# Attention and expert-mixture kernel on one core: every step issued in a newly listed order

## The chip, the cores and the metric

The kernel runs on one core of a Trainium2 chip. A core has five engines, each with a queue of its own that is worked off strictly in order: TensorE (PE in the profile, with its weight loads as PEld), VectorE (DVE), ScalarE (ACT), GpSimd (POOL) and SyncE (SP), which here only issues transfers. The metric is the device time of one execution in microseconds, as a median of several runs.

## The reference, cut to what matters

Two layers follow each other. The first is linear attention over 8 batches of 8 heads with 576 positions; the second takes its output as `x` and mixes four causal attention experts, of which each position uses two.

```python
def phi(x):
    proj = np.einsum('bhsd,df->bhsf', x, w_phi)
    proj = proj - np.max(np.abs(proj), axis=-1, keepdims=True)
    return np.concatenate([np.exp(proj), np.exp(-proj)], axis=-1)
q_p, k_p = phi(q), phi(k)
kv, z = np.einsum('bhsf,bhsd->bhfd', k_p, v), np.sum(k_p, axis=2)
x = np.einsum('bhsf,bhfd->bhsd', q_p, kv) / (q_p @ z + 1e-6)      # heads side by side: 512 features
...
for e in range(4):                                               # second layer
    q, k, v = x @ wq[e], x @ wk[e], x @ wv[e]
    a = causal_softmax(q @ k.T / sqrt(64))
    out += gate[e] * (a @ v @ wo[e])                             # gate: softmax over the two best of x @ w_gate
```

## The kernel before, in words

The work of the first layer is cut into 32 pairs of heads (`p`), that of the second into 8 batches with two groups of two experts each (16 units `n`). Each part is a Python generator, called a stream here, that emits the instructions of one step and then yields the engine of its next step:

- `stream_k`, `stream_tails`: projections of the keys (L501), maximum and subtraction on VectorE (L566, L569), exponentials on ScalarE (L305).
- `stream_q`: projections of the queries (L501), copies out of PSUM, a maximum over partitions on GpSimd (L713), subtraction on VectorE (L715), exponentials on ScalarE.
- `stream_kv`: the products of keys and values (L642 with `v_in`) and the sums of the keys (L654). From pair 4 on the key sums are first added up by accumulating transfers that GpSimd issues into `zs` (L331, L582).
- `stream_n`: denominators (L740) and numerators (L751), then a division on VectorE.
- `stream_s`: projections of the second layer (L294), scores (L871), masks on GpSimd (L979), maxima (L992, L996), subtraction (L1000), exponentials, sums (L1012, L1038).
- `stream_t`: scores times values (L1067) and the output projection (L294), stored by SP.
- loads: `load_v` has one buffer, `v_in`: the load of pair `p` may begin only after the products of pair `p-1`. `q_in` and `k_in` have two buffers.

TensorE works with four tilings of its array, which the profile prints after the names: 128*128 (second-layer projections, transposes), 64*128 (first-layer projections and scores), 128*32 (all products that give 32 columns) and 64*32 (the tails, L607). A run of neighbouring groups of one tiling is followed by a change to another.

Nothing in the kernel orders the work but two literal strings. `ORDER` has one character for each of 3,118 steps; the character's code minus 48 is the place, in the list of streams still open, of the stream that steps next. A stream that ends leaves the list, and a new one (a copy out of PSUM, say) is appended. `SIDES` has one digit for each of 520 copies that either ScalarE (0) or VectorE (1) can make.

```python
for c in ORDER:
    s = self.streams[ord(c) - 48]
    if isinstance(st.eng, tuple):
        st.eng = st.eng[int(next(sides))]
    slot = sorted(self.psum[st.tag], key=lambda kt: self.last.get(kt[0], (0.0, ''))[0])[:st.n]
```

The costs in `class Plan` (`run`, `transfer`, `blocked`, `change_cost`) decide nothing here but which of the eight free PSUM banks a step takes: the one whose last use the costs put earliest. `in_order` makes each engine keep the listed order. `keep_warm` issues 21 small matmuls in seven steps, on data that no result uses.

Of the kernel before, what the change touches and what calls it, by code (L numbers as in the profile page):

```python
# [45 lines left out]
WARM = 0   # L46
# [22 lines left out]


ORDER = (
    r'1110049B32894DDBBDCB726C8D99E1B8DF7GD4FEHDH000C=EDBF5CBBB9DC1934DEFE==E98H2=HIHHCED168E<=A541F<77DBIFJCEAE6AHH'
    r'HIC93941HB<D<E<AGBC<===G<E9GGDAGGDCF9529<GD6GH9B48KEI13F<0;7EA6CKCECG@<<BIH<B;B8IGJE8?A@EF:AE57C7@A2J:?JHHF:18'
    r'6830ADEBDB;;;BFC6CC277GGE?LF?K@FBF2G@8::3BIHEF;;:DIH@?:5ADHIGBF7:HGH::EB;?FAEEE76C8C@CJI>IC?B0;<<<<95IE884B8FB'
    r'F9F<GHH02IEGHAB3?966B>81;A>8=8CB6EB9E99BD>A=>DABAAAB;88C8A?8841>;7CC;@G5?7EEJC>D;3;88KIJODEDDJICHBB;;;;;AF80:E'
    r'FFBCE>?EHEH;AAG:6FF?DC8DD8D;2;5C@@ACBBB8:MIJBI::<IAGIC@FBH99F869FHDB8DCECB83CFBFBC088=DFEECBC8:68I8BFF70HG7IID'
    r'CG8D?5=B<GH6C4:99B2ECMEBEJA8J9886=GJD?>778CMI<HJKI>I<I@<BG39E9C18IHE<A@=8=?E?9G8857?7?EHAJJF083882HGF8ICDHC8DD'
    r'998:C6:GJHI>?I<:JG<1J:7IGH7J:KJGD:?<<BB:BE>@C>;GIIF>L;8>GJGIIJ;8<:=8:HJGHGGJ:IF::LGGK?I=N8=5:=>@K802GQJMM>F:I<'
    r':<0CEEBK=CFE::CFDCDDCJBICDCJCE=D9;;IJHJ<ICIKFHDF4883DD<8<G<<=BBBEI=CCDCDGEFEHGE8BB8D6A8>:I<C5:@@JJ@JEECIAD6BFI'
    r':JK:9FLH9MCLCIJGDHAF9BFAHD8IHBCIE880DH=28BHCB9;ADA@@CA@C@AEL@HB=ECD9;JJBBJD<BGFC;38772J7GF88GG?K=FD<CF895?==A3'  # L80
    r'=8EB888E67FE18D@KHJ@<0E@BCB28=E9988BBDIJID8DGB8848AF<B6<6EE57:7::G=HICLHE3DJDI:::;<BJGC>HD9GHG>B>GADEAF>EEE=8D'
    r'880@C?=B:98:DAF6DIEH8G8GBD9<:::GHHG7BB?NICL5H7B6N=EE;BGC@FI;G=E9?BDJEEBA:<::MGKKDBCG:GC=CD@BIGLMGKFBJH<G:=1348'
    r'8>?EI8IHCA=B;C<<<B>B28>:8:>>>JD>DL8DCBFKJE8::C=<FKEA5G8@:<=HFJHH9<>99AM=6HD?EK==K3@88028K7CJCLFNMKD>?<F?8G887?'
    r'26I88I<AGCC?KJBG<?G=99?8F>H?>F88883AH?E9=I5=F170GIJ@EIKG<=A<DE=HE<7LDB9=<M808<;;C<C6FDCDA99<GGDJ8G@KK7DL85N2GB'
    r'38JGNMGNMHFE?GAG6F><<7:::48E:FF8F8CDFB=E:E:FIJKJ>8FCCCI89B9JIBHI>8:FDDC@D88A::EA3D7F:LFHK8:<II7PHFG?A?@KL@H=5B'
    r'KNN8:6::MPOAMAOGE;E:80:F28E241AKLIJIIFAEEB08=B>ECE8EF:;;89GHH8@@>?5HE6?HI?IHCFBE?B<<<<<GE6BDB>AC?E=CBCB?>:9;@9'
    r'JJ>>A89E=:GJGLKGJ@38087J<887F=88G8LKC:?8G?:KHL<FJH@69@9P95SADQNOQ3A8788O8OMQQPR<@NQN<MEB889ADF>HCIAJB>=99II>GD'
    r'E8<H2=CD8<FFCD7AA7888?D7FCJEA?0?812:503D4=>GA?EBI::H:<BLNELK6:ACBH6K9GAJG9A?I7I7<JH<HF??IAG?NJHIL<GM::<<E@>J28'
    r'88>FE8?A6KKGCFIJFG5MIK8;@EL;N3KPK8L:<NQNL>;:8L:84F0RP=L@:>>OPK:K:FO@KAF:::8LPMKHDFNFG:HFGLKJMK<IGGEEGE=E82CEDC'
    r'FDCC;E;D8F89::I;FL8LF=GGEC5:HN:<<=L=PDOSJBBJDE@<IBJ<DA<BEIMI?F=D9KE99AB01886OCEJGCE6IKACJAM>FDEBGLJGBHMFA@>883'  # L90
    r'@<I?FCB<DH<A888IG8875AGI7IDCMDE>IEK>C>BFCJ=<B??A?D999FFGE8GFEE3088882A8FFC<677F8GF8FA999AG6E<818248>I?EHJK7H<H'
    r'7ED5A>MFIENN>NEDFHE6HK388A<FFFC>DGG:;:99GDG;::::IHK<CJ<GFJKL??FFIKJEH8CB6I;DFKKDFJJ8:8<:::JJNMM8>57:GKBGQ6FP::'
    r'::HQRBD@3880808>E@R>K@C8HIKC=ID:HDEBFDBDBBDCADBBBHHG1<C@7875::9BCBA9C@@7AB<A64?@I;L?KA?HC?L?@IJ<G>;>F;;;==ACAB'
    r'F>DIE9KH9G9?FBBH<IFC;82=8FC73=M@D117B?B778M0;;;MJ@>JMLN>6IJBG9;=6@A>J?HCEG>6@6@@<46DEE53>G;;?>DAG;5II@:E?B=A:;'
    r'A;;797B>66660056CDF>D:B9C9DB<B9B668BA<3CB583B?A4;B@@?8;533BCB:@4A?<8=2224;B?@C;@6=2024C?64111336331D;F>DF?C5C1'
    r';CCC>?:133A?C93B5@3AD3AB39FB@C<78AA3>C?:9?3?B;=8<29@;?><?<A>><211877A;:A>=;>4;42;A3C<1=C?C>@000:8;?::>:7@75008'
    r'8;<4444=475EB<0C:007222?5>=822CF41;@18@;7?777D:9:;;;:01>679==6636800;<=B?95?04<7;761=000>6=6>><=89=54002<;<9;3'
    r'9:77674734607420224700<;02232=5722901>::509;7761008866838<8:50:97086880500100:8865857757957:996657161660005?=='
    r'90064444=A=7<71=1??119;588::276679;697672141125541121171101141311114144;;322=2:1591427717235100230553431131212'
    r'100=>45210<<0;;01168224224344034023200'  # L100
# [17 lines left out]
class Plan:  # L118
# [4 lines left out]
    def __init__(self):  # L123
        self.warm, self.busy = False, []
        self.tiling = None
        self.rings = [0.0, 0.0]
# [30 lines left out]
    def run(self, eng, cost, w=(), r=(), rows=128, tiling=(128, 128), port=False):
# [15 lines left out]
        if eng == 'POOL' and port:
            t = max(t, self.pairs + 215.0)
        if eng == 'POOL' and self.shared[0] < t < self.shared[1]:
            t = self.shared[1]
# [1015 lines left out]
```

## Time and profile before

| | us |
|---|---|
| median of three runs | 584.94 |
| range of the runs | 583.61 to 585.01 |
| span of the profiled execution, first to last instruction | 582.0 |
| TensorE busy in it | 568.9 |
| VectorE busy in it | 533.0 |
| ScalarE busy in it | 454.3 |
| GpSimd busy in it | 290.3 |

The profiled execution has a span of 582.0 us; what lies outside the span brings it to the run's time, 2.9 us by the median. An engine's busy time counts its instructions, not the issuing of transfers. A matmul's end is modelled, so that small gaps between pipelined matmuls don't show as idle: the distance between the starts of neighbouring groups is the better measure of what a group takes.

### The profile page before, as it was taken

The page shows a single profiled execution, that of the slowest core. Times are in us where ns is not written, and L with a number is a line of the kernel's source. Part 1 is how long each engine was busy: PE and PEld are TensorE (multiplying, and loading weights), DVE is VectorE, ACT ScalarE, POOL GpSimd, SP SyncE. Part 2 cuts the span into 40 slices and gives each one's busy share as a digit, 9 for nine tenths or more (in the row PEclk, how much of TensorE's full clock was granted, in tenths as well). Part 3 has the DMA queues.
Part 4 walks back from the last instruction along what each step waited for, and adds up shares of the span by engine and source line. Part 5 has one row for each costly group of instructions (what it writes and reads, how often), then busy time and mean ns, then how long its engine had stood idle before and what let it go on. Part 6 is the DMA issues. An engine that isn't in the chain of part 4 may idle for free.

```text
span 582.0 us, 19187 instructions
## 1 busy us (share of the span) xinstructions
PE 568.9 (98%) x7655; PEld 439.9 (76%) x7655; DVE 533.0 (92%) x1150; ACT 454.3 (78%) x1109; POOL 290.3 (50%) x223
## 2 busy tenths in 40 slices
PE   7998999999999999999999999999999999999997
PEld 5664797678785779667876878867888677878886
DVE  7999899999999998999898989989999998898894
ACT  4999888878897969868878877979778678677562
POOL 3737472666336474465554466446635367331430
PEclk9999999999999999999999999999999999999999
DMA  6579656653445753593664663565646432311012
GB/s 164 151 180 212 119 119 141 148 116 95 95 122 136 180 121 55 139 229 76 153 139 102 156 133 107 100 156 134 131 125 148 116 87 46 89 57 43 1 56 110
DMA packets 55049, 69.74 MB, mean 120 GB/s; under 512 B 29232, under 2 KB 32688, under 8 KB 54960
## 3 DMA queue, kind: packets, MB, share of 16 engines
q1 hardware_dynamic: 48368, 49.58, 29.3%
q0 software_dynamic: 6272, 18.35, 19.9%
q8 instruction: 60, 0.98, 0.7%
q10 hardware_dynamic: 320, 0.59, 0.4%
q14 instruction: 29, 0.24, 0.1%
HBM read 35.59 MB, written 14.55 MB: 86 GB/s over the span
## 4 chain that ended last, share of the span: by engine, by line
PE 86%; DVE 6%; DMA 4%; ACT 2%; issue 1%; SPq 0%; ACTq 0%; DVEq 0%
PE ps_c L294 31%; PE ps_c L501 10%; PE ps_c L751 10%; PE ps_c L642 10%; PE ps_c L1067 7%; PE ps_c L871 7%; PE ps_c L740 5%; DMA v_in<-in_v_dram 2%; PE ps_c L654 2%; PE ps_c L607 2%; DVE s L1000 1%; DMA q_in<-in_qt_dram 1%; PE ps_c L1038 1%; DVE u L715 1%; DVE max L1012 1%
## 5 line engine op out<-in xcount | busy, mean ns | idle before, releaser
L713 POOL PARTITION_ALL_REDUCE mx<-u x64 | 145.1, 2289 | 68.2 <-DVE s L1000 17.5
L294 PE MATMUL ps_c<-x,qk 128*128 128x256 f32 (+1 forms) x768 | 108.0, 298 | 0.6 <-DVE yl L298 0.6
L294 PEld LDWEIGHTS ps_c<-x,qk 128*128 128x128 f32 x768 | 102.7, 189 | 4.4 <-issue 0.9
L996 POOL PARTITION_ALL_REDUCE max<-top x16 | 57.7, 3605 | 39.3 <-DVE top L992 18.1
L979 POOL TENSOR_SCALAR_AFFINE_SELECT s<-s 128x256 f32<-128x256 f32 (+1 forms) x80 | 46.4, 626 | 57.3 <-ACT s L303 45.3
L305 ACT ACTIVATE ek<-ek 128x1024 f32<-128x1024 f32 x64 | 67.9, 1061 | 8.0 <-DVE ek L569 7.3
L303 ACT COPY s<-ps_c 64x64 f32<-64x64 f32 (+4 forms) x141 | 52.9, 434 | 17.7 <-PE ps_c L871 17.4
L1000 DVE TENSOR_TENSOR s<-s,max 128x1152 f32<-128x1152 f32 (+4 forms) x80 | 65.5, 853 | 0.6 <-POOL max L996 0.6
L642 PE MATMUL ps_c<-ek,v_in 128*32 128x256 f32 x1024 | 61.7, 381 | 2.2 <-DMA v_in<-in_v_dram 2.2
L305 ACT ACTIVATE s<-s 128x384 f32<-128x384 f32 (+4 forms) x80 | 57.7, 742 | 7.4 <-DVE s L1000 7.1
L294 PE MATMUL ps_c<-yh,wo 128*128 128x256 f32 (+1 forms) x256 | 52.9, 300 | 0.0
L331 POOL DMA_DIRECT2D zs<-ekt x28 | 23.7, 845 | 58.3 <-DVE zs L582 22.4
L642 PEld LDWEIGHTS ps_c<-ek,v_in 128*32 128x32 f32 x1024 | 31.5, 110 | 25.4 <-DMA v_in<-in_v_dram 2.9
L303 ACT COPY u<-ps_c 128x256 f32<-128x256 f32 (+1 forms) x107 | 40.5, 401 | 11.4 <-PE ps_c L501 10.9
L715 DVE TENSOR_TENSOR u<-u,mx 128x576 f32<-128x576 f32 x64 | 48.9, 779 | 0.4 <-POOL mx L713 0.4
L294 PE MATMUL ps_c<-vg,x 128*128 128x260 f32 x384 | 49.0, 285 | 0.2 <-ACT s L303 0.2
L331 POOL DMA_DIRECT2D zs<-ek x28 | 25.4, 906 | 46.1 <-ACT ek L305 29.6
L294 PEld LDWEIGHTS ps_c<-vg,x 128*128 128x128 f32 x384 | 47.1, 188 | 1.2 <-issue 0.5
L1067 PE MATMUL ps_c<-s,vs 128*32 128x320 f32 (+4 forms) x896 | 46.8, 357 | 0.2 <-DVE ek L569 0.2
L501 PE MATMUL ps_c<-q_in,wf 64*128 64x256 f32 (+1 forms) x256 | 42.8, 430 | 3.6 <-DMA q_in<-in_qt_dram 3.2
L566 DVE TENSOR_REDUCE pmax<-ps_c 128x4 f32<-128x512 f32 x64 | 42.4, 681 | 3.8 <-PE ps_c L501 3.3
L305 ACT ACTIVATE mx<-u 128x576 f32<-128x576 f32 x64 | 43.3, 687 | 2.3 <-DVE u L715 2.0
(132 smaller groups left out, 1350.3 us busy)
## 6 DMA issues: line engine op xcount, KB each, us to landing
zs<-ek POOLq DMA_DIRECT2D x28, 512.0 KB, 5.3
out_dram<-ot SPq DMA_DIRECT2D x32, 288.0 KB, 3.0
q_in<-in_qt_dram SPq DMA_DIRECT2D x60, 144.0 KB, 3.6
k_in<-in_kt_dram SPq DMA_DIRECT2D x64, 128.0 KB, 3.4
v_in<-in_v_dram SPq DMA_DIRECT2D x32, 256.0 KB, 3.3
kvd<-kvt SPq DMA_DIRECT2D x104, 48.0 KB, 2.4
kv<-kvd SPq DMA_DIRECT2D x26, 192.0 KB, 2.5
zs<-ekt POOLq DMA_DIRECT2D x28, 128.0 KB, 3.3
```

The source lines that it names most:

```text
L294: nc.tensor.matmul(o, a, b, start=start, stop=stop, skip_group_check=True)
L303: nc.scalar.copy(o, i)
L305: nc.scalar.activation(o, i, func, **kw)
L331: nc.gpsimd.dma_start(o, i, accum_op=ALU.add)
L501: nc.tensor.matmul(o, a, b, start=True, stop=True, skip_group_check=True)
L642: nc.tensor.matmul(o[g, 0:2], v_in[:, 4 * h + t, k:64:2], ek[:, t, :, h, :].rearrange("p c (w f) -> p c w f", w=4), start=False, stop=t == ...
L713: nc.gpsimd.partition_all_reduce(M, U, 128, bass_isa.ReduceOp.absmax)
L715: dve(S, [uk], [mk], port=True).tensor_tensor(out=U, in0=U, in1=M, op=ALU.subtract)
L751: nc.tensor.matmul(ps[g:g + 32, 0:n], kvi[:, 2 * k + (h ^ p % 2), 32 * c:32 * c + 32], P_[h][c][:, s0:s1], start=c == 0, stop=c == 1, skip ...
L996: nc.gpsimd.partition_all_reduce(big.rearrange("p e s -> p (e s)"), top.rearrange("p e s -> p (e s)"), 128, bass_isa.ReduceOp.max)
L1000: dve(2 * (S - 128 * j), [('d', x, j)], [('max', z)], 1.11, True).tensor_tensor(out=block(s_, j, None, rows(j)), in0=block(s_, j, None, ro ...
L1067: nc.tensor.matmul(ps[r:r + 32, q0 - s0:s1 - s0], vs[:, j, 128 * g + 64 * e + k:128 * g + 64 * e + 64:2], ss[x][:, e, o + q0:o + s1], star ...
```

## The change

Both strings are replaced, with the same lengths of 3,118 and 520. The steps are the same on each stream, in the same order within a stream; what differs is how the streams are interleaved, and on which engine some copies run. The seven steps of `keep_warm` are now counted (`WARMS = 7`), where the loop before ended when the first `x` was there, which was also after seven. The costs of `Plan` are changed as well (a table for changes of tiling, a normal distribution for VectorE's wait behind GpSimd, two rings for transfers), and with them the choice of PSUM banks. A default argument `p=p` is added in `stream_n`, where `p` can't have moved on by then.

```diff
-WARM = 0 
+WARMS = 7
-EXIT = 95.0
-ENTRY = {'F': 102.0, 'R': 99.0, 'S': -31.0, 'C': 23.0, 'Q': 10.0}
+CHANGES = {'CR': 160.0, 'CS': 160.0, 'CF': 190.0, 'CQ': 220.0, 'FC': 100.0, 'FQ': 90.0, 'FR': 95.0, 'FS': 92.0, 'RF': 105.0, 'RC': 100.0, 'RS': -85.0, 'RQ': 105.0,
+           'SR': 50.0, 'SF': 118.0, 'SC': 118.0, 'SQ': 136.0, 'QC': 255.0, 'QR': 245.0, 'QF': 245.0, 'QS': 255.0}
...
 ORDER = (
-    r'1110049B32894DDBBDCB726C8D99E1B8DF7GD4FEHDH000C=EDBF5CBBB9DC1934DEFE==E98H2=HIHHCED168E<=A541F<77DBIFJCEAE6AHH'
...
+    r'11112221111307@16ABAA@7A02@5@BCB776F64;05ABD@DC2B7B7CJ@BI@3;FDCCECC1277@;@EDGB0F6;@I@5;KKB<@EAKGHGJDG@3E;DAF6;'
...
 SIDES = (
-    r'11110000111111000000001000011100000000110101100000001010001000000010010000110000000000000010000000000000000000'
...
+    r'11100000000100100000001000111000000000011000000001101000000000000000000100000000000000000000000000000000000000'
...
-        while ('x', WARM, PARTS[1][0]) not in done:
+        for _ in range(WARMS):
             yield Step('PE')
```

Read character by character against the streams' steps, the two strings give these orders. Each engine but VectorE and ScalarE has as many steps as before: TensorE 658, GpSimd 219, SP 297.

Neighbouring TensorE groups of different tiling (A: 128*128, B: 64*128, C: 128*32, D: 64*32):

| from, to | A B | A C | A D | B A | B C | B D | C A | C B | C D | D B | D C | all |
|---|---|---|---|---|---|---|---|---|---|---|---|---|
| before | 12 | 23 | 9 | 30 | 27 | 4 | 14 | 43 | 3 | 6 | 10 | 181 |
| after | 7 | 21 | 9 | 26 | 19 | 6 | 11 | 40 | 1 | 4 | 12 | 156 |

Within B, a projection of the first layer directly before or after a group of scores: 24 times before, 44 after.

Copies on VectorE: 73 before, 55 after. Those on ScalarE: 447 and 465. The difference of 18 is mostly copies out of PSUM of 256 to 320 columns, `u` (6), `s` (4), `kkh` (4) and `ot` (3).

The `keep_warm` steps: before, three at the head of TensorE's list, three behind the key projections of pair 1 (L501), one behind the transposes of pair 2 (L665); after, all seven at the head.

TensorE work listed between the end of one pair's L642 products and the start of the next pair's, where it is under 5.5 us (each sum made of the start-to-start durations of such groups in the trace of the kernel before, as all sums of listed work here): before, pair 1 4.9, pair 5 4.2 and pair 13 5.1; after, pair 1 4.9, pair 2 5.3, pair 3 4.4, pair 11 4.9 and pair 21 4.6. Pairs 5 and 17 have 4.2 and 9.8 us before, 10.8 and 13.5 after.

TensorE work listed between the last step on another engine and the TensorE step that uses its result, as a median: exponentials of a query pair to its denominators, 3.9 us before and 6.9 after; last add into `zs` to its use, 5.1 and 6.4; `y` to the output projection, 3.2 and 6.8; last sum on VectorE to L1038, 1.8 and 2.8; exponentials of a key pair to L642, 14.4 and 13.3.

## Rows read from the trace of the kernel before

**Rows 1.** The page's first part: busy us, share of the span, instructions.

```profile
PE 568.9 (98%) x7655; PEld 439.9 (76%) x7655; DVE 533.0 (92%) x1150; ACT 454.3 (78%) x1109; POOL 290.3 (50%) x223
```

**Rows 2.** Windows: length, busy us of each engine (instructions), granted clock, DMA share, GB/s.

```profile
9.00:560.00 551.00, 546.78 (x7384) 420.69 (x7381) 513.66 (x1087) 442.75 (x1080) 289.73 (x219) 1.00 0.51 120
...
9.00:40.00 31.00, 30.49 (x531) 20.48 (x531) 30.04 (x60) 29.45 (x56) 19.51 (x12) 1.00 0.61 163
80.00:160.00 80.00, 79.51 (x1038) 62.22 (x1039) 76.28 (x156) 65.80 (x160) 43.20 (x35) 1.00 0.54 121
```

**Rows 3.** Waits of TensorE: who waited for whom, total us, times, longest.

```profile
PE ps_c L501 <- DMA q_in<-in_qt_dram: 3.2, 2, 3.0
PE ps_c L642 <- DMA v_in<-in_v_dram: 2.2, 2, 1.7
```

**Rows 4.** Timeline of TensorE's matmuls, 302 to 324 us: start, length, line, operands, tiling, count.

```profile
302.60 0.67 PE L740 MATMUL ps_c<-mx,kv 128*32 128x288 f32 x8
...
303.68 0.39 PE L871 MATMUL ps_c<-qh,kkh 64*128 64x256 f32 x2
...
307.92 0.42 PE L871 MATMUL ps_c<-qh,kkh 64*128 64x320 f32 x2
...
308.46 0.36 PE L871 MATMUL ps_c<-qh,kkh 64*128 64x448 f32 x2
...
312.65 1.16 PE L501 MATMUL ps_c<-wf,k_in 64*128 64x128 f32 x16
313.65 0.60 PE L501 MATMUL ps_c<-q_in,wf 64*128 64x256 f32 x4
...
318.18 0.70 PE L740 MATMUL ps_c<-mx,kv 128*32 128x288 f32 x8
...
319.15 0.43 PE L654 MATMUL ps_c<-zs,ones 128*32 128x128 f32 x8
...
322.91 1.06 PE L501 MATMUL ps_c<-wf,k_in 64*128 64x128 f32 x16
323.89 1.33 PE L294 MATMUL ps_c<-x,qk 128*128 128x256 f32 x9
```

**Rows 5.** The same timeline, 363 to 385 us.

```profile
363.12 1.05 PE L501 MATMUL ps_c<-wf,k_in 64*128 64x128 f32 x16
363.92 0.39 PE L871 MATMUL ps_c<-qh,kkh 64*128 64x320 f32 x2
...
364.44 0.36 PE L871 MATMUL ps_c<-qh,kkh 64*128 64x448 f32 x2
...
383.73 1.06 PE L501 MATMUL ps_c<-wf,k_in 64*128 64x128 f32 x16
384.62 0.71 PE L501 MATMUL ps_c<-q_in,wf 64*128 64x320 f32 x4
```

**Rows 6.** The chain that ended last, at two places: start, us, what it waited on.

```profile
50.25 5.73 DMA v_in<-in_v_dram
...
247.40 6.25 DMA v_in<-in_v_dram
```

**Rows 7.** Timeline of GpSimd before those two places: issues of accumulating transfers.

```profile
48.92 0.89 POOL L331 DMA_DIRECT2D zs<-ek  x1 [1.19 <-ACT ek L305]
...
245.45 0.89 POOL L331 DMA_DIRECT2D zs<-ek  x1 [3.83 <-ACT x L303]
```

**Rows 8.** The tile v_in, all 32 loads: from issue to landing.

```profile
DMA to landing us min/median/max: 2.5/3.3/6.3
```

**Rows 9.** Groups by line and shape: a VectorE copy; ScalarE's longest exponential, from the page.

```profile
L315 DVE COPY u<-ps_c 128x320 f32<-128x320 f32 x11 | 5.2, 481 | 0.4 <-PE ps_c L501 0.4
...
L305 ACT ACTIVATE ek<-ek 128x1024 f32<-128x1024 f32 x64 | 67.9, 1061 | 8.0 <-DVE ek L569 7.3
```

**Rows 10.** Timeline of TensorE at the start: the small matmuls of keep_warm.

```profile
1.06 1.14 PE L294 MATMUL ps_c<-warm 128*128 128x128 bf16 x9 [1.06 <-DVE col L338]
...
11.51 0.68 PE L294 MATMUL ps_c<-warm 128*128 128x128 bf16 x9
```

More of the change, by code (lines that the diff above doesn't have):

```diff
@@ L1 @@
+import math
 from contextlib import ExitStack
@@ new lines, in expected, with shape_kind @@
+def expected(x, hold):
+    x = 4.0 * math.floor(x / 4.0 + 0.5)
+    if not -2400.0 <= x < 5792.0:
+        return 0.0
+    a, b = (hold - x) / SPREAD, (-LEAD - x) / SPREAD
+    below, at = (lambda z: 0.5 * (1.0 + math.erf(z / 2 ** 0.5))), (lambda z: math.exp(-0.5 * z * z) / (2 * math.pi) ** 0.5)
+    return max(0.0, (hold - x) * (below(a) - below(b)) + SPREAD * (at(a) - at(b)))
+def shape_kind(t):
+    return ('C' if t[0] == 128 else 'Q') if t[1] < 128 else 'F' if t[0] == 128 else 'S' if len(t) > 2 else 'R'
@@ L64, in change_cost @@
 def change_cost(a, b):
-    if a is not None and a[:2] == b[:2]:
+    if a is None or a == b:
         return 0.0
-    kind = ('C' if b[0] == 128 else 'Q') if b[1] < 128 else 'F' if b[0] == 128 else 'S' if len(b) > 2 else 'R'
-    return EXIT + ENTRY[kind]
+    return CHANGES[shape_kind(a) + shape_kind(b)]
 ORDER = (
-    r'1110049B32894DDBBDCB726C8D99E1B8DF7GD4FEHDH000C=EDBF5CBBB9DC1934DEFE==E98H2=HIHHCED168E<=A541F<77DBIFJCEAE6AHH'
-    r'HIC93941HB<D<E<AGBC<===G<E9GGDAGGDCF9529<GD6GH9B48KEI13F<0;7EA6CKCECG@<<BIH<B;B8IGJE8?A@EF:AE57C7@A2J:?JHHF:18'
@@ L74 @@
[L74 to L78, printed above, removed]
@@ L134, in __init__ @@
         self.pairs = 0.0
+        self.issued = False
         self.done = set()
@@ L151, in clocked, with blocked @@
         return 2 * cost if slow else cost
-    def blocked(self, t):
-        return max([b - t for a, b in self.pool if a < t < b], default=0.0)
+    def blocked(self, t, cost):
+        late = 0.0
+        for a, b, lo in self.pool:
+            if b - a > 1000:
+                late = max(late, expected(t - a, b - a))
+            elif lo < t < b:
+                late = max(late, b - t)
+        if self.pool and not self.issued and t < self.pool[-1][0] and late <= 200.0:
+            self.free['POOL'] += max(0.0, t + cost - self.pool[-1][0] - 140.0)
+        return late
     def run(self, eng, cost, w=(), r=(), rows=128, tiling=(128, 128), port=False):
@@ L169, in run @@
         if eng == 'DVE' and port:
-            cost += self.blocked(t)
+            cost += self.blocked(t, cost)
             self.shared = (t, t + cost)
             self.pairs = t + cost
[L173 to L176, printed above, removed]
+        if eng == 'POOL':
+            if port:
+                t = max(t, self.pairs + 215.0)
+            if port > 1000 and self.issued:
+                lo = t - 250.0 if t - self.free[eng] < 60 else t
+            else:
+                if self.shared[0] < t < self.shared[1]:
+                    t = self.shared[1]
+                lo = t
         end = t + cost
@@ L194, in transfer @@
         self.free[eng] = t + issue
+        if eng == 'POOL':
+            self.issued = True
         ring = int(eng == 'POOL')
-        self.rings[ring] = max(self.rings[ring], t + issue + 650.0) + cost
-        end = self.rings[ring] + (1500.0 if ring else 1150.0)
+        lead, rate, tail, share = RINGS[ring]
+        (a, b), (c, d) = self.rings[ring], self.rings[1 - ring]
+        x = max(b, t + issue + lead)
+        if x > b:
+            a = x
+        b = x + cost * rate
+        if c <= x < d:
+            b = min(x + cost * rate / share, d + max(0.0, cost * rate - share * (d - x)))
+        self.rings[ring] = (a, b)
+        end = b + tail
         for k in r:
@@ L741, in stream_n @@
                                          P_[h][c].rearrange("p (a b i) -> p b a i", b=2, i=32)[:, half], start=c == 0, stop=c == 1, skip_group_check=True)
-            plan.spawn(fractions('d', p, ps, pk, 1e-6, xf, ['xf'], (lambda: all(('xd', p - 1, s0) in done for s0, s1 in PARTS)) if p else None, ('rb', p)))
+            plan.spawn(fractions('d', p, ps, pk, 1e-6, xf, ['xf'], (lambda p=p: all(('xd', p - 1, s0) in done for s0, s1 in PARTS)) if p else None, ('rb', p)))
             for s0, s1 in PARTS:
```

67 lines of the change are left out of this document (38 added, 29 removed).

## The prediction

> **What bounds the kernel now.** I read the page's first part, then the windows, then TensorE's waits, then TensorE's timeline. The first part shows TensorE busy for 98% of the span, VectorE for 92%, ScalarE for 78% and GpSimd for 50% [rows 1]. The windows show where TensorE's 13.1 us of idle time are: between 9 and 560 us it is busy for 546.78 of 551.00 us, so only 4.2 us are idle there [rows 2]; the other 8.9 us are the start, where 3.2 us are waits for the first query loads [rows 3], and the end, where the last outputs are copied and stored. Of the 4.2 us in the middle, 2.2 us are two waits for `v_in` [rows 3]. A better order can thus win little by filling idle time. But a busy TensorE isn't TensorE at its peak, so I looked into the busy time next, by the distance between the starts of neighbouring groups: there a change of tiling can be seen, and this is what a list decides.
>
> **What a change of tiling costs.** The denominators (L740) take 319.15 - 318.18 = 0.97 us when 128*32 work follows, and 303.68 - 302.60 = 1.08 us when 64*128 work follows: leaving a tiling costs 0.11 us [rows 4]. Key projections (L501) between others of 64*128 take 384.62 - 383.73 = 0.89 us [rows 5]; entered from 128*32 they take 313.65 - 312.65 = 1.00 us, so entering 64*128 costs 0.11 us; left for 128*128 they take 323.89 - 322.91 = 0.98 us, so leaving costs 0.09 us [rows 4]. I take 0.10 us for leaving and 0.11 us for entering. For entering 128*128 I take the same 0.11 us as for 64*128, the nearest row, with bounds of 0 and 0.2 us. Entering 128*32 or 64*32 isn't shown alone; it lies between 0 and the same 0.11 us, and I take 0, the end that gives the change less.
>
> Projections and scores share the tiling 64*128. A projection between two groups of scores takes 363.92 - 363.12 = 0.80 us, and the scores behind it 364.44 - 363.92 = 0.52 us, together 1.32 us [rows 5]. Apart, the projection takes 0.89 us [rows 5], and the same scores take 308.46 - 307.92 = 0.54 us when entered from 128*32, of which 0.11 us is the entry [rows 4]: 0.89 + 0.43 = 1.32 us. So such neighbours cost nothing, and the new list has 44 of them for 24.
>
> **The change part by part.** The two lists, read against the streams, have 181 and 156 changes of tiling. By kind: into 128*128 or 64*128 from the large tilings there are fewer by 5 + 4 + 3 + 3 = 15 (A to B, B to A, C to A, C to B), at 0.10 + 0.11 = 0.21 us each 3.15 us. Into 128*32 there are fewer by 2 + 8 = 10 (A to C, B to C), at 0.10 us each 1.0 us. Those that touch 64*32 nearly cancel: two fewer from C to D, two more from B to D, two fewer from D to B at 0.11 us, two more from D to C at 0: 0.2 us. The sum is 4.35 us, say 4.4 us less. With entering 128*128 at 0 instead it is 3.6 us; with entering 128*32 at 0.11 us and entering 128*128 at 0.2 us it is about 6 us. All of it lies on TensorE's own queue, and between 9 and 560 us TensorE is idle for only 0.8% of the time, so nothing hides it: it comes off the span unless something else is late.
>
> **Loads of `v_in`.** The chain shows two loads of 5.73 and 6.25 us which ended it [rows 6], each issued 1.3 to 2.0 us after an accumulating transfer into `zs` [rows 7]; the median load lands after 3.3 us and the slowest after 6.3 [rows 8]. They are those of pairs 5 and 17, with 4.2 and 9.8 us of TensorE work listed for cover. The new list gives them 10.8 and 13.5 us, more than the slowest landing. The 2.2 us of waits go. What is late next is another short cover: five pairs (1, 2, 3, 11, 21) have 4.4 to 5.3 us, together 24.1 us. At the median landing none of them waits; were all as slow as the slowest, they would wait 5 x 6.3 - 24.1 = 7.4 us. Pairs 1 to 3 are loaded before any transfer into `zs`, pair 11 has none listed near it and pair 21 one well ahead, so I take the end near the median and charge 1.0 us for these and for every other new wait together. The median covers of query exponentials, `zs`, `y` and the VectorE sums all grow, by 1.0 to 3.6 us; that of the key exponentials shrinks from 14.4 to 13.3 us, against a ScalarE exponential of 1.06 us [rows 9]. This speaks against a larger charge.
>
> **Copies and warm-up.** Eighteen copies go from VectorE to ScalarE. At 0.48 us each as in the row for 320 columns, VectorE gets 8.7 us less [rows 9]; neither engine ends the chain for long, so I count it at nothing. The cover is TensorE's own work; where it is gone, see the second rival. Of the 21 small matmuls, nine stand in TensorE's time at 11.51 us, 0.6 to 0.7 us long, and now run at the head, in the wait for the first load, where the first nine took 1.14 us [rows 10]. They were filling a wait for ScalarE, so moving them brings between 0 and 0.7 us; I take 0. The new costs in the planner change only the choice of PSUM banks, which I count at nothing; a bad choice would be a wait of one copy, about 0.5 us [rows 9], and has no likely sign.
>
> The sum against the profiled execution: 582.0 - 4.4 - 2.2 + 1.0 = 576.4 us. The 2.9 us outside the span, by the median, stay: **579.3 us**.
>
> **The rivals.** First: the same, and the remaining waits shrink too, because the covers grew. What is left in the middle is 4.2 - 2.2 = 2.0 us, and the charge of 1.0 us isn't due, with 0.7 us from the warm-up: 579.3 - 3.7 = 575.6 us. For it speaks the table of covers; against it that the start and the end, where most of the idle time is, look much alike in both lists.
>
> Second: VectorE sets the pace. Between 80 and 160 us it is busy for 76.28 of 80 us [rows 2], 95%, and part of that is waiting inside its instructions. Then the 4.4 us come back as TensorE's idle time and only the `v_in` waits may be won: 584.9 - 2.2 + 1.0 = 583.7 us. Against it: VectorE loses 8.7 us of copies, and TensorE didn't wait for it in the stretches where VectorE was fullest (79.51 of 80 us busy) [rows 2].
>
> Third, slower: ScalarE holds the PSUM banks. The 18 copies now stand in its queue behind exponentials of up to 1.06 us [rows 9], and it is already busy for 29.45 of 31 us between 9 and 40 us [rows 2]. A bank comes free later, and TensorE waits at its next group. If ten of the eighteen held TensorE for one exponential each, the time would be 579.3 + 10.6 = 589.9 us. It gets slower than before by over 0.3% from seven such waits on, 7 x 1.06 = 7.4 us. Against it: before, TensorE's waits for `v_in` and the query loads alone are 5.4 us [rows 3] of the 13.1 us that it is idle at all, though 447 copies are already made on ScalarE. The Trainium skill speaks for this rival (TensorEngine Tiling (Array Packing), section PSUM Bottleneck): it says that tiling doesn't speed up the emptying of PSUM, and that both ScalarE and VectorE should share the copies. The rows of before don't show that bound yet.
>
> Fourth: the list doesn't do what was counted, because the changes of tiling overlap with other work more than in the few places that I read. Then only the waits change, by -2.2 + 1.0: again about 583.7 us.
>
> **How the numbers follow.** The forecast has a chance of 0.50, the first rival 0.16, the second 0.12, the third 0.14 and the fourth 0.08. A measurement of this kernel can tell about 0.3% from no change, 1.75 us, so faster means under 583.2 us and slower over 586.7 us. The forecast and the first rival are faster, as are a quarter of the second and fourth: 0.66 + 0.05 = 0.71. The third is slower in all but its mildest cases: 0.13. The same is left with 0.16. The range reaches from 575.0 us, just under the first rival, to 587.0 us: the forecast with all of the 7.4 us at the `v_in` loads is 579.3 - 1.0 + 7.4 = 585.7 us, and a milder third rival still lies inside.
>
> **What would show it.** Right: TensorE's busy time falls to about 564 us and its idle time between 9 and 560 us stays under 5 us; the wait of L642 for `v_in` is gone or under 1 us; VectorE's busy time falls by some 8 us and ScalarE's rises by as much. Wrong: TensorE's busy time stays at 569 us (fourth); it falls while waits for VectorE grow (second); waits of TensorE for ScalarE's copies of `u`, `s` or `kkh` of several us appear (third); long `v_in` loads at pairs 1 to 3, 11 or 21. A median over 587 us would mean that waits which the list alone doesn't show outweigh everything that I counted.

## The result and the profile after

The changed kernel took 588.66 us (median of 19 runs, 585.23 to 591.40), the kernel before 584.84 us beside it (19 runs, 583.61 to 585.81). The ratio is 1.0068 with a 95% interval of 1.0051 to 1.0084: slower by 0.7%, where the forecast was 579.3 us with a range up to 587.0 us. The profiled execution took 588.19 us, with a span of 586.4 us against 582.0 us before. The 2.9 us that the description above puts outside the span before are too many: in all 72 runs of that kernel beside the experiments the time is 1.7 to 1.9 us over the span.

Line numbers of the changed file are higher by 42 (L740 is L782, L751 is L793, L642 is L684, L654 is L696, L501 is L543). First the part of the page that answers [rows 1], then TensorE's waits, which answer [rows 3] (total us, times, longest):

```profile
PE 569.4 (97%) x7655; PEld 445.3 (76%) x7655; DVE 528.3 (90%) x1130; ACT 458.1 (78%) x1129; POOL 287.8 (49%) x223
```

```profile
PE ps_c L782 <- DMA kv<-kvd: 4.2, 2, 4.0
PE ps_c L1003 <- DVE col L994: 2.0, 1, 2.0
PE ps_c L684 <- DMA v_in<-in_v_dram: 1.8, 1, 1.8
PE ps_c L543 <- DMA q_in<-in_qt_dram: 1.2, 1, 1.2
...
PE ps_c L793 <- ACT ot L345: 1.0, 1, 1.0
PE ps_c L696 <- DMA zs<-ekt: 0.9, 2, 0.7
```

TensorE's busy time is not lower but higher by 0.5 us, and two waits are new or longer: 4.0 us for `kv` in the denominators (L782), for which TensorE didn't wait before, and 2.0 us for the last gate (L1003; 0.8 us before). The windows around these two show a second thing (columns as in [rows 2]; the number behind GpSimd's is the granted clock):

```profile
160.00:174.50 14.50, 14.50 (x184) 10.78 (x182) 13.71 (x34) 13.42 (x39) 4.09 (x8) 1.00 0.54 125
174.50:178.50 4.00, 0.04 (x6) 0.04 (x3) 1.32 (x3) 2.30 (x7) 3.58 (x1) 1.00 0.97 218
178.50:182.00 3.50, 3.50 (x33) 2.09 (x37) 1.40 (x5) 0.85 (x4) 0.00 (x0) 0.52 0.33 107
...
567.40:571.00 3.60, 3.60 (x68) 2.47 (x72) 3.39 (x8) 1.47 (x6) 0.00 (x0) 0.55 0.24 89
```

From 174.5 to 178.5 us TensorE does nothing, and for the next 3.5 us it is busy without a gap but at a mean granted clock of 0.52, nearly all of it the lower level of 1.2 GHz: 3.5 x 0.48 = 1.7 us are lost once more. Behind the gate's wait it is the same, 3.6 x 0.45 = 1.6 us. Such time counts as busy, which hides it from the first part of the page; in the profiled execution before, between 9 and 560 us, the clock was 1.00 [rows 2].

**Where the 4.4 us of span came from.** I took the distances between the starts of neighbouring groups of TensorE, subtracted for each kind of group its undisturbed distance (from the short ones of before) and the prices of the changes of tiling, and summed what was left. This is a reckoning with my prices and no view of the profile. What the groups take undisturbed is the same in both kernels, 528 us. The changes of tiling take 29.1 us before and 24.7 us after: 4.4 us less, as in the sum. The rest, waits and slow clock, takes 18.6 us before and 27.8 us after: 9.2 us more. (What is left of the two spans, 6.3 and 5.9 us, stands ahead of the first group and behind the last.) So the gain is there and more than twice of it was given back. The experiments ask what gave it back, and whether the 4.4 us, which rest on prices of mine, are real.

**How the wait for `kv` comes about.** SyncE's queue in the changed kernel (start, us from first to last of the group, what is moved):

```profile
147.88 1.96 SPq L369 DMA_DIRECT2D kvd<-kvt  x4
163.35 0.36 SPq L369 DMA_DIRECT2D out_dram<-ot  x1
163.75 1.59 SPq L369 DMA_DIRECT2D kt_in<-in_kt_dram  x2
165.38 0.61 SPq L369 DMA_DIRECT2D v_in<-in_v_dram  x1
166.04 3.25 SPq L369 DMA_DIRECT2D vt_in<-in_v_dram  x4
169.33 1.23 SPq L369 DMA_DIRECT2D q_in<-in_qt_dram  x2
170.68 0.52 SPq L369 DMA_DIRECT2D out_dram<-ot  x1
171.30 0.37 SPq L369 DMA_DIRECT2D kv<-kvd  x1
```

and two steps of the chain that ended last (start, us, what):

```profile
171.30 7.06 DMA kv<-kvd
...
178.49 2.06 PE ps_c L782 x16
```

The queue stands from 149.8 to 163.35 us at `store 0.0` (`out_dram<-ot`), which waits for ScalarE's copy of `ot`. Behind it four loads and another store go out one after the other, and `kv<-kvd` of pair 11 is the last of them, at 171.30 us. It lands 7.06 us later, where the median of these loads is 2.6 us; an accumulating transfer into `zs`, issued at 170.51 us, runs beside it, and the DMA share between 174.5 and 178.5 us is 0.97. TensorE came to the denominators of pair 11 at 174.5 us. At the median landing `kv` would have been there at 173.9 us, so the wait took both: the late issue and the long landing.

The store's hold isn't new. Before, SyncE stood at the same store from 147.8 to 164.88 us, and the load of `kv` for pair 11 went out at 175.06 us, but TensorE wanted it only at 182.26 us:

```profile
164.88 0.34 SPq L327 DMA_DIRECT2D out_dram<-ot  x1
...
175.06 0.34 SPq L327 DMA_DIRECT2D kv<-kvd  x1
```

What the new list changed is what stands behind the store, and how soon it is wanted.

The Trainium skill (DMA: Bandwidth & Descriptors, section Anatomy of one DMA — SWDGE (gpsimd) path) says that a DMA's wait on a semaphore happens on the issuing sequencer, before dispatch. The rows agree: 13.5 us pass at one store, and all that is listed behind it goes out later. (The section is on the path of transfers that GpSimd issues; the rows are of SyncE's.)

### The profile page after: what moved, and what is told of

It is laid out like the page before. It is cut to its first block, busy times and chain, and to the rows that moved or that the text cites. A ratio compares the mean times of both kernels' runs of the same rounds, so it can differ in the third digit from the quotient of the medians.

```text
span 586.4 us, 19178 instructions
## 1 busy us (share of the span) xinstructions
PE 569.4 (97%) x7655; PEld 445.3 (76%) x7655; DVE 528.3 (90%) x1130; ACT 458.1 (78%) x1129; POOL 287.8 (49%) x223
## 4 chain that ended last, share of the span: by engine, by line
PE 74%; ACT 8%; DMA 6%; DVE 4%; POOL 3%; issue 2%; SPq 2%; ACTq 0%; POOLq 0%; DVEq 0%
PE ps_c L336 30%; PE ps_c L543 10%; PE ps_c L793 8%; PE ps_c L684 7%; PE ps_c L1109 6%; PE ps_c L913 6%; PE ps_c L782 4%; SPq L369 2%; DMA kv<-kvd 2%; POOL mx L755 2%; ACT ek L347 1%; DMA zs<-ekt 1%; PE ps_c L649 1%; PE ps_c L1080 1%; ACT mx L347 1%
## 5 line engine op out<-in xcount | busy, mean ns | idle before, releaser
L755 POOL PARTITION_ALL_REDUCE mx<-u x64 | 141.4, 2243 | 62.8 <-ACT u L345 18.4
L336 PE MATMUL ps_c<-x,qk 128*128 128x256 f32 (+1 forms) x768 | 106.5, 298 | 0.0
L336 PEld LDWEIGHTS ps_c<-x,qk 128*128 128x128 f32 x768 | 102.4, 189 | 3.3 <-ACT u L345 0.9
L1038 POOL PARTITION_ALL_REDUCE max<-top x16 | 57.3, 3582 | 59.0 <-DVE top L1034 29.8
L1021 POOL TENSOR_SCALAR_AFFINE_SELECT s<-s 128x256 f32<-128x256 f32 (+1 forms) x80 | 48.9, 647 | 58.6 <-ACT s L345 56.0
L684 PE MATMUL ps_c<-ek,v_in 128*32 128x256 f32 x1024 | 62.4, 384 | 1.8 <-DMA v_in<-in_v_dram 1.8
L347 ACT ACTIVATE s<-s 128x640 f32<-128x640 f32 (+4 forms) x80 | 57.4, 743 | 5.2 <-DVE s L1042 5.1
L345 ACT COPY u<-ps_c 128x320 f32<-128x320 f32 (+1 forms) x113 | 42.4, 405 | 22.4 <-PE ps_c L543 21.8
L345 ACT COPY s<-ps_c 128x512 f32<-128x512 f32 (+4 forms) x147 | 54.0, 433 | 7.2 <-PE ps_c L913 6.9
L684 PEld LDWEIGHTS ps_c<-ek,v_in 128*32 128x32 f32 x1024 | 32.7, 111 | 26.4 <-issue 5.1
L336 PE MATMUL ps_c<-yh,wo 128*128 128x320 f32 (+1 forms) x256 | 52.4, 299 | 0.1
L336 PE MATMUL ps_c<-vg,x 128*128 128x260 f32 x384 | 49.3, 285 | 0.0
L1109 PE MATMUL ps_c<-s,vs 128*32 128x320 f32 (+4 forms) x896 | 48.5, 366 | 0.0
L336 PEld LDWEIGHTS ps_c<-vg,x 128*128 128x128 f32 x384 | 47.1, 188 | 1.2 <-ACT vs L345 0.4
L1109 PEld LDWEIGHTS ps_c<-s,vs 128*32 128x32 f32 x896 | 30.5, 113 | 19.5 <-issue 1.3
```

Source lines behind the costliest of these rows:

```text
L336: nc.tensor.matmul(o, a, b, start=start, stop=stop, skip_group_check=True)
L345: nc.scalar.copy(o, i)
L347: nc.scalar.activation(o, i, func, **kw)
L684: nc.tensor.matmul(o[g, 0:2], v_in[:, 4 * h + t, k:64:2], ek[:, t, :, h, :].rearrange("p c (w f) -> p c w f", w=4), start=False, stop=t == ...
L755: nc.gpsimd.partition_all_reduce(M, U, 128, bass_isa.ReduceOp.absmax)
L1021: nc.gpsimd.affine_select(out=d, in_=d, pattern=[[0, 2], [1, w]], compare_op=ALU.is_ge, fill=FILL, base=0, channel_multiplier=-1)
```

## The experiments

All kernels named a_ are the changed kernel with its PSUM tiles pinned to those that it had (where not said otherwise), so that an edit moves only the steps that it names.

**One place at a time.** Four kernels move one suspect each, or all three. The edits, by the names of the steps:

```diff
a_kv11 (SyncE)
 kvd<-kvt 11
+kv<-kvd 11
 store 0.0
 load t 7, load v 12, load vt 6, load q 14, store 0.1
-kv<-kvd 11
a_v9 (SyncE)
+load v 9
 load vt 5, load t 6
-load v 9
a_tail (ScalarE; VectorE)
+copy s 256 15
 copy v 260 7.1, copy v 260 7.0
-copy s 256 15
+gate2 7
 sub s15.0 ... sub s15.4
-gate2 7
```

a_kv11, expected:

> The changed kernel, its PSUM banks written out literally; on SP alone the load of kv for pair 11 is listed 12 transfers earlier, directly behind the four transfers that fill its source. Theory 1 (a few long waits took the gain, and TensorE's clock fell to half behind the longest): the wait of 4.0 us for kv goes, and with it one stretch at a granted clock of 0.5, 1.7 us: 588.7 - 5.7 = 583.0 us. Theory 2 (the loss is spread over hundreds of small waits, and the next one takes the place of any that is removed): 587.0 to 588.7 us.

Measured: 589.12 us, ratio 1.0089 (1.0058 to 1.0121). No gain. One line of SyncE's waits and two of TensorE's tell why:

```profile
SPq L369 <- PE ps_c L793: 16.4, 3, 15.4
```

```profile
PE ps_c L782 <- DMA kv<-kvd: 3.4, 1, 3.4
PE ps_c L649 <- DMA vt_in<-in_v_dram: 3.2, 2, 2.7
```

The moved load now holds the queue itself, for 15.4 us, because its buffer is one of two and the numerators (L793) of pair 9 still read it; behind it the load of `vt` 6 goes out at 170.88 us, where it went out at 166.04 us in the changed kernel, and TensorE waits for that one, at the same place, with half the clock behind the wait. The wait for `kv` that is left is another, at about 470 us.

a_v9, expected:

> The changed kernel, banks written out; on SP alone the load of v_in for pair 9 is listed ahead of six small loads (vt_in, kt_in). Theory 1: the wait of 1.8 us for v_in at 110 us goes, no clock change there: 588.7 - 1.8 = 586.9 us. Theory 2: 588.0 to 589.0 us, since the small loads come later instead.

Measured: 587.83 us, 1.0044 (1.0011 to 1.0077). The wait for `v_in` is gone from TensorE's waits, and the median is 0.8 us lower, where 1.8 us were expected; the intervals don't part this from nothing.

a_tail, expected:

> The changed kernel, banks written out; in the last 30 us one ScalarE copy of scores goes ahead of two copies of v, and VectorE's end of the last gate calculation goes ahead of its five last subtractions. Theory 1: TensorE's wait of 2.0 us for the gate goes and so does the stretch at half clock behind it (1.7 us): up to 3.7 us less, 585.0 us. Theory 2 (VectorE's chain of the last unit sets the end, whichever wait TensorE has): only the earlier copy counts, 0.4 to 1.8 us: 587.0 to 588.3 us.

Measured: 591.7 us, 1.0109 (1.0071 to 1.0148). No gain, but 3.0 us more than the changed kernel, in four runs. The gate no longer waits, but the sums behind it do:

```profile
PE ps_c L1080 <- DVE max L1054: 2.4, 1, 2.4
```

I read this as VectorE's chain ending late as a whole, so that moving one link ahead of another only chose who waits; no run parts this from other readings. The profiled execution also has a third stretch at half clock, behind a wait of 1.9 us at 256 us, far from the edit, so the 3.0 us need not be the edit's alone.

a_three, expected:

> The three edits together. Theory 1: 588.7 - 5.7 - 1.8 - 1.8 to 3.7 = 577.5 to 579.4 us, so that the fewer changes of tiling show, faster than the kernel before by about 1%. Theory 2: not under 584 us.

Measured: 588.79 us, 1.0072 (1.0047 to 1.0097). Theory 1 in this form has fallen: three named waits are taken away and the time stays. What replaced them, though, is late for the same reason at the first place (3.3 us for `vt_in` behind the held queue, again with a slow clock behind it). So the suspect became the queue and not the one load.

**The queue as a whole, the tail as a whole, and the clock by itself.** Four more:

```diff
a_sp (SyncE)
 kvd<-kvt 11
+load vt 6, load v 12, load t 7, load q 14
 store 0.0
+kv<-kvd 11
-load t 7, load v 12, load vt 6, load q 14
 store 0.1
-kv<-kvd 11
a_tail2: from "scores0 14" on, all engines' steps in the order of before
a_all2: a_sp + a_v9 + a_tail2
a_fill: in the den product of pair 11, ahead of its matmuls
+for _ in range(62): mm(ps[:, 0:128], warm, warm, ...)
  and in the gate product of block 7
+for _ in range(30): mm(ps[:, 0:128], warm, warm, ...)
```

a_sp, expected:

> The changed kernel with its PSUM banks as they are; only on SyncE's queue, around the first store, transfers change places: the loads of vt 6, v 12, t 7 and q 14 go ahead of store 0.0 (their buffers are free since about 146 us), and the load of kv 11 goes right behind it, ahead of store 0.1. Theory 1 (the 4.0 us wait for kv at 174 us and the 3.4 us stretch at half clock behind it come from the queue that store 0.0 holds until 163 us): 588.7 - 4.0 - 1.7 = 583.0 us, and no wait of TensorE above 1 us between 160 and 185 us. Theory 2 (the list is so tight that whatever is mended, another transfer or engine is late next at the same place): 587 to 589 us, with a wait of 3 us or more for another tile there.

Measured: 582.62 us, 0.9966 (0.9948 to 0.9983): under the kernel before, and 6.0 us under the changed one, from the order of seven steps. SyncE's queue and the windows of the same stretch:

```profile
150.65 2.39 SPq L369 DMA_DIRECT2D vt_in<-in_v_dram  x4
153.14 1.66 SPq L369 DMA_DIRECT2D v_in<-in_v_dram  x1
154.89 1.33 SPq L369 DMA_DIRECT2D kt_in<-in_kt_dram  x2
156.27 1.26 SPq L369 DMA_DIRECT2D q_in<-in_qt_dram  x2
163.64 0.36 SPq L369 DMA_DIRECT2D out_dram<-ot  x1
167.37 0.32 SPq L369 DMA_DIRECT2D kv<-kvd  x1
```

```profile
174.50:178.50 4.00, 4.00 (x102) 2.67 (x92) 3.62 (x12) 2.85 (x10) 3.56 (x2) 1.00 0.46 126
178.50:182.00 3.50, 3.50 (x50) 2.80 (x50) 3.45 (x5) 3.45 (x10) 1.23 (x3) 1.00 0.81 158
```

The store still waits until 163.6 us, but four loads whose buffers were free went out ahead of it. `kv` goes out at 167.37 us, as soon as its buffer is free, ahead of the `zs` transfer, and lands in 2.4 us. TensorE has no gap and no slow clock there. Theory 1 said 583.0 us. The wait of 2.0 us at the last gate is still there, but in this profiled execution no slow clock follows it, so up to 1.6 of the 6.0 us may not be the queue's.

a_tail2, expected:

> The changed kernel up to the score products of block 14 (about 535 us), PSUM banks as they are until there; from there on every engine's steps in the order of the kernel before. Theory 1 (the end is late by its own order: ScalarE's copies of block 15's scores behind exponentials, VectorE's four additions of block 14 ahead of the maxima of block 15): the wait of 2.0 us ahead of the last gate falls to the 0.8 us of before, and with it the half clock behind it goes: 588.7 - 1.2 - 1.7 = 585.8 us. Theory 2 (the end is late because it is entered late on VectorE and ScalarE): 588 to 589 us, and the same wait of 2 us or another near 565 us.

Measured: 589.74 us, 1.0084 (1.0051 to 1.0117). The gate's wait fell to 0.8 us as before, and the time did not fall: in its profiled execution the end runs at full clock, but a stretch at half clock follows the wait of 1.7 us for `v_in` instead:

```profile
113.00:116.50 3.50, 3.50 (x40) 1.95 (x44) 1.96 (x5) 3.44 (x6) 1.95 (x1) 0.53 0.37 101
```

The tail's own worth can't be read from this run.

a_all2, expected:

> The edits of the two kernels beside it and the load of v 9 ahead of vt 5 and t 6 (which took the wait of 1.8 us for v_in away). Theory 1 (the loss is these three places, each with its price and the half clock behind it, while the 25 fewer changes of tiling give 4.5 us): 588.7 - 5.7 - 1.8 - 2.9 = 578.3 us, under the 585.0 us of before. Theory 2 (new waits take their places): 584 us or more, with waits of TensorE of 2 us or more that the changed kernel did not have.

Measured: 581.63 us, 0.9954 (0.9927 to 0.9981). Both `v_in` and the tail together bring 1.0 us over a_sp, not 4.7: theory 1 is right in sign and on the queue, and too high for the rest.

a_fill, expected:

> The changed kernel with its list and banks as they are; TensorE gets 62 more matmuls of keep_warm's form (128x128, bf16) right ahead of the den product of pair 11, into its own PSUM tile, and 30 ahead of the last gate product, so that it works through most of the waits of 4.0 and 2.0 us there. The waits themselves stay (the filler is about 3.5 and 1.7 us long). Theory A (the half clock follows an idle TensorE and costs 1.7 us each time): both stretches at half clock go, 588.7 - 3.4 = 585.3 us, mean granted clock of 0.999 or more. Theory B (the half clock comes from something else, and the idle time ahead of it is chance): 588 to 589.5 us, clock 0.993 as in the changed kernel.

Measured: 586.17 us, 1.0024 (1.0003 to 1.0045), mean granted clock 1.000. The same windows as in the changed kernel:

```profile
174.50:178.50 4.00, 3.90 (x70) 3.46 (x62) 1.07 (x4) 1.04 (x5) 3.55 (x1) 1.00 1.02 247
178.50:182.00 3.50, 3.41 (x90) 2.25 (x90) 2.50 (x7) 2.88 (x10) 0.03 (x1) 1.00 0.51 152
...
567.40:571.00 3.60, 3.60 (x88) 2.68 (x84) 3.39 (x9) 1.11 (x5) 0.00 (x0) 1.00 0.24 89
```

The filler does no work for the result and ends where the wait ended, yet the time is 2.5 us lower (3.4 expected): the half clock follows TensorE's idle time, and is a cost of its own beside the wait.

**Prices.** Four kernels on the base of a_all2 or of the changed kernel, and a fifth:

```diff
x_sw, in each num256 product of pairs 8 to 31, after half of its matmuls (128*32)
+mm(ps[:, 384:512], warm, warm, ...)        # 128*128
x_same, in each out256 product of blocks 0 to 5, after half of its matmuls (128*128)
+mm(ps[:, 384:512], warm, warm, ...)        # 128*128
a_best (a_all2, and on SyncE)
+store 1.0
 load vt 9, load q 19, load v 17, load t 10
-store 1.0
a_banks (the changed kernel, tiles not pinned)
-slot = sorted(self.psum[st.tag], key=lambda kt: self.last.get(...))[:st.n]
+slot = self.psum[st.tag][:st.n]
r_sw (a_best, TensorE), at 12 places:
-kvz 24
 projq256 25
+kvz 24
```

x_sw, expected:

> The mended kernel (the transfers around store 0.0, load v 9 and the tail of before, measured at 581.6 us) with 24 single matmuls of keep_warm's form (tiling 128*128, bf16, 128 columns) more, one in the middle of each num256 product of pairs 8 to 31, whose matmuls are of tiling 128*32, into unused columns of the same PSUM tile: 48 more changes of tiling. Theory 1 (a change costs what the prediction took from the traces, about 0.2 us: 0.11 + 0.10 into and out of either, and the matmul itself 0.06): 24 x (0.34 to 0.42 + 0.06) = 9.6 to 11.5 us, so 591 to 593 us. Theory 2 (a change of tiling is not paid for as such; the 4.5 us that left the groups were the chance of neighbours): 24 x 0.06 = 1.4 us, 583.0 us.

x_same, expected (its added matmuls change the running sums of out256 in blocks 0 to 5; the work that is timed is the same):

> The same 24 matmuls in the same mended kernel (581.6 us), but in the middle of the out256 products of blocks 0 to 5, whose matmuls are of their own tiling (128*128): no change of tiling is added. Both theories: 581.6 + 24 x 0.06 = 583.0 us. If it comes out above 585 us, the extra matmuls cost by themselves and the kernel beside it says nothing of tiling.

Measured: x_sw 587.81 us, 1.0062 (1.0040 to 1.0083); x_same 583.78 us, 0.9978 (0.9963 to 0.9994). The difference is 4.0 us for 48 changes, 0.08 us each. A change of tiling seems to cost time, but neither theory's number fits. One of the 24 places in x_sw (the added matmul is L336):

```profile
316.34 0.61 PE L793 MATMUL ps_c<-mx,kv 128*32 128x256 f32 x8
316.89 0.23 PE L336 MATMUL ps_c<-warm 128*128 128x128 bf16 x1
317.05 0.64 PE L793 MATMUL ps_c<-u,kv 128*32 128x256 f32 x8
```

The added matmul is short and of another type than the kernel's own, and in x_same it makes its neighbours 0.12 us later without any change of tiling; what part of the 0.3 us at each place in x_sw is the change can't be told cleanly. Hence r_sw, with the kernel's own products:

> The mended kernel with store 1.0 early (580.3 us) with 12 pairs of neighbours on TensorE's list exchanged (a kvz or den product, tiling 128*32, with the projt, projq256 or scores0 product behind it, tiling 64*128), so that two groups of either tiling become four: 24 more changes of tiling among the kernel's own products; PSUM tiles stay with their products, and the other engines' lists are the same. Theory 1 (the prediction's price, 0.10 us on leaving and 0.11 us on entering a tiling, 0.21 us a change): 580.3 + 24 x 0.21 = 585.3 us. Theory 2 (the price that the added matmuls showed, 0.08 to 0.10 us a change): 580.3 + 2.0 to 2.4 = 582.3 to 582.7 us. A wait that an exchange brings shows in the trace at its place, and the twelve stretches can be compared with the same stretches of the kernel without the exchanges: 0.42 us longer each by theory 1, about 0.2 us by theory 2.

Measured: 584.07 us, 0.9986 (0.9971 to 1.0001), against 580.33 us for a_best: 3.7 us for 24 changes, 0.16 us each, between the two theories; so a change of tiling does cost time. The place of `kvz` 24 (L696) and `projq256` 25 (first row of L543), in a_best and then in r_sw:

```profile
376.63 1.94 PE L684 MATMUL ps_c<-ek,v_in 128*32 128x256 f32 x32
378.38 0.40 PE L696 MATMUL ps_c<-zs,ones 128*32 128x128 f32 x8
378.72 1.24 PE L543 MATMUL ps_c<-q_in,wf 64*128 64x256 f32 x8
379.79 1.06 PE L543 MATMUL ps_c<-wf,k_in 64*128 64x128 f32 x16
```

```profile
378.51 1.94 PE L684 MATMUL ps_c<-ek,v_in 128*32 128x256 f32 x32
380.38 0.70 PE L543 MATMUL ps_c<-q_in,wf 64*128 64x256 f32 x4
381.01 0.42 PE L696 MATMUL ps_c<-zs,ones 128*32 128x128 f32 x8
381.36 0.81 PE L543 MATMUL ps_c<-q_in,wf 64*128 64x320 f32 x4
382.01 1.06 PE L543 MATMUL ps_c<-wf,k_in 64*128 64x128 f32 x16
```

From the start of `kvm` to the start of the next key projection it is 379.79 - 376.63 = 3.16 us against 382.01 - 378.51 = 3.50 us: 0.34 us for two changes. Ten of the twelve places give 0.33 to 0.34 us; the other two hold a wait each. My expectation for theory 1 was worked out wrongly: it charged 0.21 us to every change, while the prediction charged that only for entering 64*128, and 0.10 us for entering 128*32. By the prediction's own prices twelve exchanges are 12 x (0.21 + 0.10) = 3.7 us, which is what was measured.

The Trainium skill (TensorEngine Tiling (Array Packing), section Key Properties) says that a change of tiling mode drains TensorE, without a price. The trace agrees in that a change takes time, 0.17 us between products of this kernel; it doesn't show a drain as such.

a_best, expected:

> The mended kernel (581.6 us) with one more edit on SyncE's queue: store 1.0 goes ahead of the loads of vt 9, q 19, v 17 and t 10, behind which it was issued at 245.6 us while ScalarE waited 2.35 us for its landing and TensorE 1.2 us for ScalarE. Theory 1 (order in the queue is the whole of such a wait): that wait goes, 581.6 - 1.2 = 580.4 us. Theory 2 (another item of the queue is late next): 581.5 us or more, with a new wait within 30 us of that place.

Measured: 580.33 us (4 runs, 580.10 to 580.59), ratio 0.9922 (0.9900 to 0.9944): faster than both kernels, by 0.8% against before. In a_all2 ScalarE waited 2.35 us for `store 1.0` to land and TensorE 1.2 us for ScalarE; in a_best the store goes out at once, and TensorE's longest wait is down to 1.2 us:

```profile
237.63 1.01 SPq L369 DMA_DIRECT2D out_dram<-ot  x2
238.69 4.46 SPq L369 DMA_DIRECT2D vt_in<-in_v_dram  x4
```

```profile
PE ps_c L543 <- DMA q_in<-in_qt_dram: 1.2, 1, 1.2
PE ps_c L782 <- ACT ek L347: 1.1, 1, 1.1
```

a_banks, expected:

> The changed kernel with its list and nothing else changed but the choice of PSUM tiles: the one that was released first in the list, in place of the one whose last work the planner puts earliest; 458 of 519 choices differ. Theory 1 (the choice does nothing beyond a wait here and there; the waits that made the kernel slower come from the queue of transfers and stay): 587.5 to 590 us, with the wait of about 4 us for kv at 174 us still there. Rival (part of the loss is TensorE waiting for PSUM tiles that the planner's costs chose badly): under 587 us, or, if the planner's choice is what keeps ScalarE's copies off the path, above 591 us.

Measured: 594.78 us, 1.0174 (1.0146 to 1.0202), beyond theory 1 and on the rival's upper side. The wait for `kv` at 174 us, which theory 1 wanted to see again, isn't there in the profiled execution. It has small waits for other engines' copies and subtractions where the changed kernel had none, for example:

```profile
PE ps_c L913 <- DVE ek L611: 1.4, 1, 1.4
PE ps_c L782 <- DVE x L340: 1.3, 1, 1.3
...
PE ps_c L543 <- ACT u L345: 0.7, 2, 0.5
```

The listed waits add up to 13 us, as in the changed kernel; TensorE's busy time is 3.1 us higher (572.5 against 569.4 us), and what makes it so isn't shown. So the choice of PSUM tiles is worth 6 us between a choice by expected times and one by the order of release alone. It isn't needed to explain the loss, since a_sp keeps the changed kernel's choice and is under the kernel before. What the changed planner costs did by themselves, against those of before, was not separated.

## Why the prediction was wrong

**Changes of tiling: right.** The sum had 4.4 us for 25 changes. r_sw confirms the prices on the kernel's own products, for changes between 64*128 and 128*32; those into 128*128 weren't tested apart. And a_best has 156 changes and 19.2 us of waits and slow clock by the same reckoning, against 181 and 18.6 us before [rows 4, 5]: its span, 577.9 us, is 4.1 us under that of before. The fourth rival is out, and so is the first, since the waits grew.

**Loads of `v_in`: right for the two waits, wrong for what is late next.** The waits of pairs 5 and 17 [rows 6] are gone. The new one of 1.8 us is at pair 9, none of the five pairs that I named as short. I measured a cover as TensorE's work between a load's place in the list and its use; the load of pair 9 stands behind `kv` 7, `vt` 5 and `t` 6 on SyncE's queue and was issued 5 us after its buffer came free.

**The 1.0 us for every other new wait: this step failed.** In its place stand 9.2 us more of waits and slow clock. In the profiled execution these are above all the 4.0 us for `kv` 11, 1.2 us more at the last gate, the 1.8 us for `v_in`, which takes nearly the place of the old 2.2 us, and 1.7 + 1.6 us at half clock. Four things were wrong in it. I compared median covers, of which four of five grew and among which the loads of `kv` weren't, but a wait comes from the shortest one: between the load of `kv` 11 and its use the new list leaves 2.6 us of TensorE's work, where the old one left 4.1. I took a transfer to go out at its place in the list, without following SyncE's queue past the store that holds it. I took the landing near the median of 3.3 us [rows 8], though the two long landings in my own rows [rows 6, 7] stand beside `zs` transfers, and here it was 7.06 us. And an idle TensorE was priced at its idle time alone. a_sp shows the first place to be worth up to 6.0 of the 9.4 us between forecast and median; a_best shows that with the queue mended, and the end in the order of before, the list gives 580.3 us, near the forecast.

**Copies: right in effect, but the sign was badly chosen.** VectorE's busy time fell by 4.7 us, not 8.7, and ScalarE's rose by 3.8 us. The copies themselves have the size that I gave them: added up one by one, VectorE's at this line (L315, L357) took 33.2 us before and 25.4 us after, and ScalarE's (L303, L345) 209.1 and 217.8 us, so 7.8 us less and 8.6 us more. Records of neighbouring instructions overlap, and the busy time counts what overlaps once. Neither engine's copies stand among the large waits. The second rival is out, and the third, the only one that was slower, is right in sign and wrong in its cause: TensorE's waits for ScalarE in the middle are 1.0 us and less. The Trainium skill (TensorEngine Tiling (Array Packing), section PSUM Bottleneck), named for it, isn't borne out by the changed kernel; in a_banks TensorE does wait for engines that still read a PSUM tile, but through the choice of tiles, and no run here shows the rate of the copies as the bound.

**Warm-up: right.** The wait for the first queries fell from 3.2 [rows 3] to 1.2 us since the small matmuls stand in it, and where nine of them stood before [rows 10], TensorE now waits 0.7 us for ScalarE: nothing won or lost that these rows show.

**PSUM tiles at nothing: not shown.** a_banks says that the term could have been several microseconds.

**The 2.9 us outside the span: misread.** By the later runs they are 1.8 us. By that, the other 1.1 us is how much quicker the profiled execution before was than the median, so the sum started from a quick execution and added what a usual one loses inside the span. That moves the forecast by little and not its sign.

**What I said would show it.** TensorE's busy time was a poor sign. It rose by 0.5 us because time at half clock counts as busy; a_sp, without it, has 566.4 us, 2.5 us less than before, and not the 564 us that I named. Why is open: r_sw raises the busy time by 3.6 us for its 24 changes (570.8 against 567.2 us in a_best), so what a change costs does show in it. The idle time between 9 and 560 us was the better sign: I had named under 5 us, and it is 8.9 us (551.00 - 542.11). The line on a median over 587 us was the true one: waits that the list alone doesn't show outweighed what I had counted.

## What to carry to other kernels

A list of steps is checked queue by queue: for each transfer ask when its issuing queue gets to it, not where it stands, and put no load with a free buffer behind a store that waits for a result. Judge a new order by its shortest covers with the slowest landing seen, not by medians, and when a wait is mended look for the next item of the same queue before calling the cause wrong. A wait of TensorE can have a second price at half clock (here 1.6 to 1.7 us each time), which the busy time hides; read the granted clock behind every gap of some length.

## What was not expected of the hardware

- Behind gaps of 4.0 and 2.0 us in the middle of dense work the granted clock fell to 1.2 GHz for about 3.5 us, at a cost of 1.7 and 1.6 us. It doesn't follow every gap: a_sp has the same 2.0 us at the last gate and no slow stretch behind it in its profiled execution. Over all fifteen profiled executions, each of the nine gaps of 2.3 to 4.2 us in the middle has such a stretch behind it, and five of the twelve from 1.70 to 2.04 us. Of the 19 executions of the changed kernel the two with a mean clock of 0.999 or more took 585.2 and 586.2 us, those with 0.990 and 0.991 took 589.2 to 591.2 us, which is most of that kernel's spread.
- The kernel before isn't free of it. Of its 72 runs beside the experiments, 33 have a mean clock of 0.997 or less and a median of 585.8 us, and 35 have 0.999 or more and a median of 583.8 us. The execution that the rows of before come from is one at 1.00, so they couldn't show this cost.
- A load that takes 2.6 us by the median took 7.06 us beside an accumulating transfer, in a window where the DMA share was 0.97. The accumulating transfer alone doesn't do it: of the 26 loads of `kv` in that trace 20 have one in flight beside them, with a median of 2.6 us as the other six; but the four that took 4.0 us or more are all among the 20. What part the transfers just ahead of it on SyncE's queue had was not separated.
- A change of tiling costs 0.17 us between the kernel's own products of 64*128 and 128*32, but a single short matmul put between others paid less, 0.08 us a change by the medians; why is open.
